# The second layer's raw weight staging and the mixed-tile stores moved from SyncE's queue to GpSimd's, with a fourth staging buffer and later places for what follows them

## The chip, the core and the metric

The kernel runs on one core of one Trainium2 chip. The metric is device time in microseconds (us) of one launch; before the change it is 1452.85 us, the median of three runs (1451.37 to 1453.06). The engines are called as the profile calls them: PE (TensorE matmul, PEld its weight loads), DVE (VectorE), ACT (ScalarE), POOL (GpSimd) and SP (SyncE). SP computes nothing here and only issues DMAs. POOL clears a few tiles and issues the other DMAs. Every engine works through its instructions in order.

## The reference

Three blocks follow one another on a batch of 8 sequences of 576 positions and 512 features.

```python
# 1: attention through 32 packed vectors p, per batch and head (64 features)
p_packed = softmax(scale * p @ k.T) @ v
x = softmax(scale * q @ p_packed.T) @ p_packed
# 2: first feed-forward, x_prev is x one position earlier
xk = mu_k * x + (1 - mu_k) * x_prev ;  xr = mu_r * x + (1 - mu_r) * x_prev
x2 = sigmoid(xr @ w_r) * (relu(xk @ w_k) ** 2 @ w_v)
# 3: positions mixed by a rank-32 product, then the second feed-forward
u = x2 + (x2.T @ U @ V).T
out = u + relu(u @ w_ch1) @ w_ch2          # 512 -> 2048 -> 512
```

The weights arrive as 64-bit floats and are made into 32-bit ones on the chip. Every large product is computed as three products of split parts (a high part and a remainder).

## The kernel before

**How the work is cut.** Attention runs over 16 units (4 batch pairs by 4 head pairs). The first 8 run at the start. The other 8 are woven into the first feed-forward. That feed-forward runs over 12 chunks of 384 positions (`chunks`, numbers 0 to 11): for each, `mix` builds xk and xr on ACT and DVE, `r_block`, `k_block` and `v_block` run the products on PE (tiles `psr`, `psk`, `psv`), and `x2_out` multiplies the result by the gate and stores the mixed tile to DRAM. `attention` is called for four units in chunk 2 and for four in chunk 5; the profile has them from about 215 us to 470 us. The second feed-forward then runs in windows, the first from about 710 us on (tile `psc`). It reads combinations of the weights, prepared earlier, from the DRAM tiles `ws_d` and `t_d` through six `ring` buffers that `load_w` fills from POOL's queue.

**The casts of the second layer's weights.** `Cast.run` is used for 2 pieces of V, 16 of `w_ch1` and 16 of `w_ch2`, from chunk 2 on, at class 3. One cast takes a `st` buffer of three and loads 512 KB of 64-bit numbers into it (the load waits for the buffer's former user). ACT then takes absolute values into tile `a` (L233), and six DVE instructions follow: a maximum on `a`, a shift into tile `m` (L264), two bit operations, a scaling of the low half into `m` (L273) and a sum into `m` (L254). Last, the 32-bit piece in `m` is stored to DRAM (`w1_d`, `w2_d`; V's go to `v_d`). There are two `m` buffers, so the shift of cast number k + 2 waits until the store of cast k has landed. Later `raw_pair` loads these pieces again, `make_ws` and `make_t` build the combinations from them, and `make_t` also runs in the first window.

**What sets the order.** The program is first recorded as operations, then `Plan.emit` places them one after another by its own estimates of times: on each engine it takes what is ready, lower class first. The finish that it assumes for a DMA is what decides where the instructions that wait for it stand on DVE, ACT and PE:

```python
clock[e] = t + (issue if e == "sp" else 1000.0)
dge = max(dge, t + issue) + gap
wire = max(wire, dge + 700.0) + dur * share
op.fin = wire + land
```

The order is fixed by this before the kernel runs, and on the chip each engine keeps it whatever happens. A DMA issue that waits for data holds up every later issue of its queue. Before the change SP issues nearly all DMAs: the attention inputs `kin`, `qin` and `vin`, the chunks' inputs, the `st` loads, and the stores of `m`, of the attention outputs and of the mixed tiles. POOL issues 308 ring loads and 16 loads of raw pieces, from 679 us on.

**Names in the profile.** The profile leaves the numbers in names out: `x_d<-x` is the store of a mixed tile, `w_d<-m` the store of a cast piece, `w_d` under `raw` its later load, `st<-in_moe_w_ch_dram` the load of a cast. `th` is the last factor of an attention unit, `pp` a tile in its middle.

Of the kernel before, what the change touches and what calls it, by code (L numbers as in the profile page):

```python
# [11 lines left out]
I32 = mybir.dt.int32  # L12
# [77 lines left out]

class Op:
    __slots__ = ("engs", "fn", "cls", "seq", "preds", "succs", "left", "end", "eng", "cost", "done", "fin", "name",
                 "group", "vt")

    def __init__(self, engs, fn, cls, seq, cost):
        self.engs, self.fn, self.cls, self.seq, self.cost = engs, fn, cls, seq, cost
# [4 lines left out]
class Plan:  # L101
# [210 lines left out]
            return self.size(o) + 100.0  # L312
        return self.add((eng,), fn, (), (out,))

    def dma(self, out, in_, cls=None, after=(), eng="sp"):
        def fn():
            o = out.get() if isinstance(out, Ref) else out
            i = in_.get() if isinstance(in_, Ref) else in_
            (self.nc.sync if eng == "sp" else self.nc.gpsimd).dma_start(out=o, in_=i)  # L319
            runs = []  # L320
            for ap in (o, i):
                n, dims = 4, list(ap.ap)
                while dims and dims[-1][0] * 4 == n:
                    n *= dims.pop()[1]
                runs.append(n)
            return o.shape[0] * self.size(o) * 4 / (358.0 if min(runs) >= 512 else 180.0)
        return self.add((eng,), fn, [in_] if isinstance(in_, Ref) else [],
                        [out] if isinstance(out, Ref) else [], cost="dma", cls=cls, after=after)


    LAT = {"pe": {"act": 197.0, "dve": 197.0, "pool": 224.0},
# [14 lines left out]
    def emit(self):  # L346
# [68 lines left out]
        while True:  # L415
            best = None
            for e in names:
                for q in (avail[e], pend[e]):
                    while q and q[0][-1].done:
                        heapq.heappop(q)  # L420
                if avail[e]:
                    t = clock[e]
                elif pend[e]:
                    t = max(clock[e], pend[e][0][0])
                else:
                    continue
                if best is None or t < best[0]:
                    best = (t, e)
            grant = None
            for i, (ready, op) in enumerate(asks):  # L430
                for b in op.group:
                    if b.free is not None:
                        t = max(ready, b.free)
                        key = (t, op.cls, op.seq, b.free)
                        if grant is None or key < grant[0]:
                            grant = (key, i, op, b)
            if grant is not None and (best is None or grant[0][0] <= best[0]):
                key, i, op, b = grant
                del asks[i]
                op.vt.bank, op.done, op.eng, op.fin = b, True, "", key[0]  # L440
                b.free, b.last = None, 0.0
                op.fn()
                finish(op)
                continue
            if best is None:
                break
            t, e = best
            q = pend[e]
            while q and q[0][0] <= t:
                ready, _, op = heapq.heappop(q)  # L450
                if op.done:
                    continue
                key = op.seq if e in ("pe", "sp") else ready
                heapq.heappush(avail[e], (op.cls, key, op.seq, op))
            while avail[e] and avail[e][0][-1].done:
                heapq.heappop(avail[e])
            if not avail[e]:
                continue
            op = heapq.heappop(avail[e])[-1]
            op.done, op.eng = True, e  # L460
            dur = op.fn(e) if op.cost == "eng" else op.fn()
            if op.cost == "dma":
                issue, gap, share, land = self.LEAD if t < self.CHUNKS else self.LOADED
                clock[e] = t + (issue if e == "sp" else 1000.0)
                dge = max(dge, t + issue) + gap
                wire = max(wire, dge + 700.0) + dur * share
                op.fin = wire + land
            else:
                if e == "act" and op.cost in ("exp", "sig") and op.cost != table:
                    dur += 1300.0  # L470
                    table = op.cost
                if e == "pe":
                    tick = int(t // self.TICK)
                    if done.get(tick - 1, 0.0) < 3060.0:
                        dur = 2.0 * dur - 3.0
                    tick = int((t + dur) // self.TICK)
                    done[tick] = done.get(tick, 0.0) + self.cols
                clock[e] = t + (max(dur - self.OVER.get(e, 0.0), 0.0) if t < self.AHEAD else dur)
                op.fin = t + dur
            finish(op)  # L480
# [4 lines left out]
def packed_attention_moe_mixer_kernel(  # L485
# [20 lines left out]
    P = 128  # L506
    DM = H * D
# [18 lines left out]
    plan = Plan(nc)  # L526
# [362 lines left out]
    class Cast:  # L889
        N = 512  # L890

        def __init__(self, es, side):
            self.st = Pool(obj=open_pool(es, "cvst", 3, side), bufs=3)
            self.tp = Pool(obj=open_pool(es, "cvtp", 2, side), bufs=2)
            self.pools = [self.st, self.tp]

        def run(self, srcs, n, put=None, parts=None, after=()):
            N = self.N
            raw = srcs[0][1].dtype != F32
            st = plan.tile(self.st, [P, N * 2], I32, "st", parts=tuple(range(len(srcs))))  # L900
            for i, (rows, src) in enumerate(srcs):
                s = st.at(i)
                to = s[rows, 0:2 * n] if raw else s[rows, 0:n].bitcast(F32)
                if raw:
                    src = src.bitcast(I32)
                if src.shape[0] > P:
                    to = to.rearrange("p (a c) -> p a c", a=src.shape[0] // P)
                    src = src.rearrange("(a p) c -> p a c", p=P)
                plan.dma(to, src, after=after)
            if not raw:  # L910
                if parts is None:
                    put(st.bitcast(F32))
# [224 lines left out]
    def x2_out(n, t):  # L1137
        b, c = chunks[n]
        i = 3 * c + t
        x2 = plan.tile(x2_p, [P, 512], F32, "x2")  # L1140
        plan.tt(x2, vps[n][t], rt.pop((n, t)), mul)
        plan.dma(x2_d[b].at(i)[:, i * DM:(i + 1) * DM], x2)
        return x2

    def xu_block(tiles):
# [61 lines left out]
    def raw_pair(src, f):  # L1207
        r = []
        for m in (2 * f, 2 * f + 1):
            t = plan.tile(st_p, [P, 512], F32, "s", name="raw")  # L1210
            plan.dma(t, src[m])
            r.append(t)
        return r

# [363 lines left out]
    CAST0, NPER, NPLAINB, FIRST_T = 2, 5, 1, 10  # L1578
    for m in range(MC):
        def put1(w, m=m):  # L1580
            plan.dma(w1_d[m], w)
        casts.append((slice(0, P), w_ch1[:, m * P:(m + 1) * P], 512, put1))
    for m in range(MC):
        def put2(w, m=m):
            plan.dma(w2_d[m], w)
        casts.append((slice(0, P), w_ch2[m * P:(m + 1) * P, :], 512, put2))

    def finish(n):
# [164 lines left out]
```

## Time and profile before

| what | value |
|---|---|
| median of the runs | 1452.85 us (1451.37 to 1453.06) |
| the profiled execution's own time | 1451.24 us |
| its span | 1449.0 us |
| PE busy | 1405.5 us, 97% |
| DVE busy | 1069.9 us, 74% |
| ACT busy | 700.8 us, 48% |
| POOL busy | 173.8 us, 12%, 340 instructions |
| hardware DMA queue (SP's issues) | 165296 packets, 171.77 MB, 40.2% of 16 engines |
| software DMA queue (POOL's issues) | 45632 packets, 165.70 MB, 38.2% of 16 engines |

PE is busy nearly all the time, so the end comes earlier only where PE waits less or runs faster. A busy share says nothing on that; the waits of PE and what released them do. A wait is listed with the engine and instruction that waited, and after the arrow with what came last. An engine that waits off PE's path costs nothing by itself, so a wait on DVE or ACT counts only as far as PE waits for its result.

### The profile page before, as it was taken

What the parts mean: (1) busy time and instruction counts of PE and PEld (TensorE: products, weight loads), DVE (VectorE), ACT (ScalarE), POOL (GpSimd) and SP (SyncE); (2) the same over time, 40 slices, a digit from 0 to 9 for tenths busy, and PEclk for the clock granted to TensorE, in tenths of its full rate; (3) what the DMA queues carried; (4) which work ended last, traced back from release to release, by engine and by line L of the source; (5) the groups of instructions that cost most, each with busy time, mean ns of one, the idle gap of its engine ahead of it and who ended that gap; (6) DMA issues with size and microseconds to landing.
All of it is one profiled execution on the core that took longest, in us unless ns stands there. A gap on an engine that the chain in (4) does not pass through costs nothing.

```text
span 1449.0 us, 25125 instructions
## 1 busy us (share of the span) xinstructions
PE 1405.5 (97%) x9256; PEld 1273.4 (88%) x9256; DVE 1069.9 (74%) x2071; ACT 700.8 (48%) x1403; POOL 173.8 (12%) x340
## 2 busy tenths in 40 slices
PE   7889998999999999999999999999999999999998
PEld 5558887887887888888898899999999999999997
DVE  6777965887887888878568756957876894696484
ACT  5667654766666666667325322422432342243232
POOL 0000000000000000000121122222222222222221
PEclk8889999999999999999999999999999999999999
DMA  8864335656655466887688799899999989999886
GB/s 232 233 194 145 110 94 135 186 160 184 185 145 175 139 226 237 286 294 231 188 277 258 229 339 293 273 288 305 310 272 303 329 242 330 298 262 288 253 252 176
DMA packets 211050, 339.07 MB, mean 234 GB/s; under 512 B 88304, under 2 KB 120880, under 8 KB 210928
## 3 DMA queue, kind: packets, MB, share of 16 engines
q1 hardware_dynamic: 165296, 171.77, 40.2%
q0 software_dynamic: 45632, 165.70, 38.2%
q8 instruction: 74, 1.21, 0.4%
q14 instruction: 48, 0.39, 0.1%
HBM read 262.87 MB, written 74.52 MB: 233 GB/s over the span
## 4 chain that ended last, share of the span: by engine, by line
PE 67%; issue 15%; DMA 7%; POOL 4%; DVE 3%; ACT 2%; SPq 1%; POOLq 0%; DVEq 0%; ACTq 0%
PE psc L197 17%; PE psv L197 12%; PE psk L197 12%; PE psr L197 7%; PE psat L197 4%; POOL ring L319 4%; PE psX L197 4%; PE psY L197 3%; PE psZ L197 2%; DMA ring<-ws_d 2%; PE psat L209 2%; DMA kin<-in_k_dram 1%; PE psW L197 1%; PE psu L197 1%; DMA w_d<-m 1%
## 5 line engine op out<-in xcount | busy, mean ns | idle before, releaser
L197 PE MATMUL psc<-ob,ring 128*128 128x384 f32 x2016 | 357.0, 335 | 2.2 <-DVE hid L254 0.9
L197 PEld LDWEIGHTS psc<-ob,ring 128*128 128x128 f32 x2016 | 349.6, 188 | 7.8 <-issue 2.7
L197 PE MATMUL psv<-w,kk 128*128 128x512 f32 x783 | 202.7, 396 | 2.3 <-DVE kk L291 2.3
L254 DVE TENSOR_TENSOR hid<-p,psc 128x384 f32<-128x384 f32 x144 | 79.1, 550 | 140.3 <-PE psc L197 140.1
L197 PEld LDWEIGHTS psv<-w,kk 128*128 128x128 f32 x783 | 144.2, 188 | 30.7 <-DVE kk L291 2.7
L288 ACT ACTIVATE p<-psc 128x384 f32<-128x384 f32 x96 | 47.2, 492 | 252.7 <-PE psc L197 247.9
L319 POOL DMA_DIRECT2D ring<-ws_d x168 | 88.9, 529 | 446.6 <-PE psc L197 244.3
L288 ACT ACTIVATE sp<-hid 128x768 fp32r<-128x768 f32 x104 | 87.9, 846 | 109.2 <-PE psX L197 54.3
L254 DVE TENSOR_TENSOR sp<-hid,sp 128x768 fp32r<-128x768 f32 x104 | 99.2, 954 | 25.4 <-ACT sp L288 25.3
L197 PE MATMUL psk<-xk,w 128*128 128x384 f32 x528 | 104.7, 341 | 0.1
L319 POOL DMA_DIRECT2D ring<-t_d x140 | 73.9, 528 | 229.3 <-PE psY L197 65.3
L197 PEld LDWEIGHTS psk<-xk,w 128*128 128x128 f32 x528 | 93.4, 189 | 5.5 <-issue 0.8
L197 PE MATMUL psX<-ring,sp 128*128 128x256 f32 x720 | 88.6, 283 | 0.8 <-DMA ring<-t_d 0.8
L197 PEld LDWEIGHTS psX<-ring,sp 128*128 128x128 f32 x720 | 87.4, 192 | 1.6 <-DMA ring<-t_d 1.6
L197 PE MATMUL psY<-ring,sp 128*128 128x256 f32 x720 | 88.0, 283 | 0.0
L197 PE MATMUL psZ<-ring,sp 128*128 128x256 f32 x720 | 88.0, 283 | 0.0
L197 PEld LDWEIGHTS psY<-ring,sp 128*128 128x128 f32 x720 | 87.1, 192 | 0.0
L197 PEld LDWEIGHTS psZ<-ring,sp 128*128 128x128 f32 x720 | 87.1, 192 | 0.0
L197 PE MATMUL psr<-wA,xr 128*128 128x512 f32 x315 | 86.9, 405 | 0.0
L233 ACT ACTIVATE sp<-hid 128x768 fp32r<-128x768 f32 x52 | 44.0, 846 | 78.7 <-PE psY L197 26.3
L233 ACT ACTIVATE sq<-psk 128x384 f32<-128x384 f32 x96 | 46.5, 488 | 62.0 <-PE psk L197 61.0
L197 PEld LDWEIGHTS psr<-wA,xr 128*128 128x128 f32 x315 | 58.8, 192 | 14.1 <-DVE xr L291 0.8
(202 smaller groups left out, 2400.1 us busy)
## 6 DMA issues: line engine op xcount, KB each, us to landing
ring<-ws_d POOLq DMA_DIRECT2D x168, 512.0 KB, 5.9
ring<-t_d POOLq DMA_DIRECT2D x140, 512.0 KB, 4.8
st<-in_moe_w_ch_dram SPq DMA_DIRECT2D x32, 512.0 KB, 4.9
ws_d<-bl SPq DMA_DIRECT2D x56, 256.0 KB, 3.5
t_d<-bl SPq DMA_DIRECT2D x56, 256.0 KB, 3.5
x_d<-xo SPq DMA_DIRECT2D x16, 576.0 KB, 3.5
x_d<-x SPq DMA_DIRECT2D x36, 256.0 KB, 2.3
kin<-in_k_dram SPq DMA_DIRECT2D x32, 256.0 KB, 5.0
```

The lines of the kernel that those rows point to most:

```text
L197: self.nc.tensor.matmul(o, l, r, start=start, stop=stop, **k)
L209: self.nc.tensor.transpose(out.get(), in_.get(), ident.get())
L233: self.nc.scalar.activation(o, in_.get(), func, **k)
L254: return self.elem(engs, lambda e, o, x, y: e.tensor_tensor(out=o, in0=x, in1=y, op=op), out, [a, b], self.TT, cls)
L288: self.nc.scalar.activation(o, i, AF.Copy)
L319: (self.nc.sync if eng == "sp" else self.nc.gpsimd).dma_start(out=o, in_=i)
```

## The change

In `Op` and `Plan.dma` a number `slack` is added that the planner adds to the finish it assumes for the DMA. On the chip nothing waits for it; what depends on the DMA is placed later. It is 4000 ns for the loads of the casts and for the stores of `w1_d` and `w2_d` pieces. For `raw_pair` it is given as 0, which changes nothing. Every fourth of these casts takes its staging buffer from the pool `xs_p` (one buffer, until then used for `u` tiles only), so there are four in turn. The casts' loads, the stores of the pieces, and the stores of the mixed tiles in `x2_out` are issued by POOL instead of SP. The stores of V's two pieces stay on SP.

```diff
-    def dma(self, out, in_, cls=None, after=(), eng="sp"):
+    def dma(self, out, in_, cls=None, after=(), eng="sp", slack=0.0):
...
+        op.slack = slack
+        return op
...
-                op.fin = wire + land
+                op.fin = wire + land + op.slack
...
+            self.count = 0
...
-            st = plan.tile(self.st, [P, N * 2], I32, "st", parts=tuple(range(len(srcs))))
+            self.count += raw and plan.cls == 3
+            pl, tag = (xs_p, "xs") if plan.cls == 3 and self.count % 4 == 0 else (self.st, "st")
+            st = plan.tile(pl, [P, N * 2], I32, tag, parts=tuple(range(len(srcs))), name="st")
...
-                plan.dma(to, src, after=after)
+                plan.dma(to, src, after=after, slack=4000.0 if plan.cls == 3 else 0.0, eng="pool" if plan.cls == 3 else "sp")
...
-        plan.dma(x2_d[b].at(i)[:, i * DM:(i + 1) * DM], x2)
+        plan.dma(x2_d[b].at(i)[:, i * DM:(i + 1) * DM], x2, eng="pool")
...
-            plan.dma(t, src[m])
+            plan.dma(t, src[m], slack=0.0)
...
-            plan.dma(w1_d[m], w)
+            plan.dma(w1_d[m], w, slack=4000.0, eng="pool")
...
-            plan.dma(w2_d[m], w)
+            plan.dma(w2_d[m], w, slack=4000.0, eng="pool")
```

36 stores of mixed tiles, 34 loads of casts and 32 stores of pieces change the queue: 102 issues leave SP and stand on POOL. What this does to the order is shown at three places. Numbers behind names are tile numbers and differ between the two programs.

The first place is chunk 2, where the first attention unit of the second group is loaded. SP before, from the loads of the next unit's keys on (`x2_d0` is a mixed-tile store, `st` a cast's load, `v_d` the store of a piece of V):

```order
L319 DMA kin_2692<-in_k_dram 128x2x256 x2
L319 DMA kin_2692<-in_k_dram 64x2x64 x2
L319 DMA qin_2693<-in_q_dram 32x18x32 x8
L319 DMA x2_d0_69<-x2_2673 128x512
L319 DMA vin_2741<-in_v_dram 128x2x256
L319 DMA vin_2741<-in_v_dram 64x2x64
L319 DMA vin_2741<-in_v_dram 128x2x256
L319 DMA vin_2741<-in_v_dram 64x2x64
L319 DMA st_2800<-in_moe2_w_ch1_dram 128x4x256
L319 DMA st_2804<-in_moe2_w_ch1_dram 128x4x256
L319 DMA v_d_77<-m_2442 32x288
L319 DMA v_d_77<-m_2483 32x288
```

SP after, at the same place:

```order
L319 DMA kin_2691<-in_k_dram 128x2x256 x2
L319 DMA kin_2691<-in_k_dram 64x2x64 x2
L319 DMA qin_2692<-in_q_dram 32x18x32 x8
L319 DMA vin_2738<-in_v_dram 128x2x256
L319 DMA vin_2738<-in_v_dram 64x2x64
L319 DMA vin_2738<-in_v_dram 128x2x256
L319 DMA vin_2738<-in_v_dram 64x2x64
L319 DMA v_d_77<-m_2442 32x288
L319 DMA v_d_77<-m_2483 32x288
```

And POOL after, where before the change there was nothing between two clearings of `x` tiles (`st_1904` is the first load into the fourth buffer):

```order
L319 DMA x2_d0_69<-x2_1905 128x512
L319 DMA st_2399<-in_moe2_V_dram 32x576
L319 DMA st_2487<-in_moe2_V_dram 32x576
L319 DMA st_2488<-in_moe2_w_ch1_dram 128x4x256
L319 DMA st_1904<-in_moe2_w_ch1_dram 128x4x256
L319 DMA x2_d0_69<-x2_2663 128x512
L319 DMA x2_d0_69<-x2_2669 128x512
L319 DMA x2_d0_69<-x2_2674 128x512
```

The two `w_ch1` loads stand side by side and ahead of the stores, and the stores of V's pieces follow the attention loads directly.

The second place is chunk 6, where the inputs of the last attention unit are loaded. SP before, with the store of a cast piece behind the attention loads and the mixed-tile stores:

```order
L319 DMA kin_5056<-in_k_dram 128x2x256 x2
L319 DMA kin_5056<-in_k_dram 64x2x64 x2
L319 DMA qin_5057<-in_q_dram 32x18x32 x8
L319 DMA x2_d1_70<-x2_4565 128x512
L319 DMA x_5135<-x_d2_67 128x4x512
L319 DMA x2_d1_70<-x2_4586 128x512
L319 DMA x2_d1_70<-x2_4589 128x512
L319 DMA w1_d13_91<-m_4771 128x512
```

POOL after, with the store of the same piece:

```order
L319 DMA x2_d1_70<-x2_4595 128x512
L319 DMA x2_d1_70<-x2_4602 128x512
L319 DMA x2_d1_70<-x2_4605 128x512
L319 DMA st_5171<-in_moe2_w_ch2_dram 128x1024
L319 DMA w1_d13_91<-m_4757 128x512
L319 DMA st_5224<-in_moe2_w_ch2_dram 128x1024
L319 DMA w1_d14_92<-m_4811 128x512
```

The store now has only stores of finished mixed tiles and one cast load ahead of it, and no attention load.

The third place is the start of the first window, with the ring loads (`ws_d0` to `ws_d5`) on POOL. Before:

```order
L319 DMA ring_7883<-ws_d0_94 128x1024
L319 DMA ring_7884<-ws_d1_95 128x1024
L319 DMA ring_7885<-ws_d2_96 128x1024
L319 DMA raw_7971<-w2_d0_122 128x512
L319 DMA raw_7996<-w2_d2_124 128x512
L319 DMA ring_7984<-ws_d3_97 128x1024
L319 DMA ring_8003<-ws_d4_98 128x1024
L319 DMA ring_8004<-ws_d5_99 128x1024
```

After:

```order
L319 DMA w2_d15_137<-m_7445 128x512
L319 DMA ring_7972<-ws_d0_94 128x1024
L319 DMA ring_7973<-ws_d1_95 128x1024
L319 DMA ring_7985<-ws_d2_96 128x1024
L319 DMA raw_8143<-w2_d0_122 128x512
L319 DMA raw_8155<-w2_d2_124 128x512
L319 DMA x2_d3_72<-x2_7815 128x512
L319 DMA x2_d3_72<-x2_7820 128x512
L319 DMA x2_d3_72<-x2_7829 128x512
L319 DMA ring_8152<-ws_d3_97 128x1024
L319 DMA ring_8163<-ws_d4_98 128x1024
L319 DMA ring_8164<-ws_d5_99 128x1024
```

The stores of the last chunk's three mixed tiles now stand between the third and the fourth ring load.

## Rows read from the trace of the kernel before

**Rows 1.** PE's waits from 190 to 740 us: total us, times, longest.

```profile
PE psat L197 <- ACT th L233: 5.2, 1, 5.2
PE psv L197 <- DVE kk L291: 2.3, 1, 2.3
PE psat L209 <- DVE pp L270: 2.1, 1, 2.1
PE psk L197 <- ACT sq L233: 0.8, 2, 0.4
PE psat L197 <- ACT ppt L288: 0.6, 1, 0.6
```

**Rows 2.** Waits of ACT and DVE for DMAs, 190 to 500 us.

```profile
ACT a L233 <- DMA st<-in_moe_w_ch_dram: 11.6, 4, 6.7
DVE m L264 <- DMA w_d<-m: 10.5, 5, 4.0
```

**Rows 3.** SP's issues in chunk 2, in order of time: start, us, instruction.

```profile
211.91 0.44 SPq L319 DMA_DIRECT2D st<-in_moe_w_ch_dram  x1
216.57 0.34 SPq L319 DMA_DIRECT2D x_d<-x  x1
...
238.49 1.09 SPq L319 DMA_DIRECT2D st<-in_moe_w_ch_dram  x2
239.67 0.92 SPq L319 DMA_DIRECT2D v_d<-m  x2
```

**Rows 4.** ACT and DVE in order of time, 243 to 246 us, idle time in brackets.

```profile
243.99 0.66 ACT L233 ACTIVATE a<-st 128x512 f32<-128x512 f32 x1 [6.71 <-DMA st<-in_moe_w_ch_dram]
...
245.61 0.43 DVE L264 TENSOR_SCALAR m<-a 128x512 int32<-128x512 int32 x1 [0.42 <-DMA v_d<-m]
```

**Rows 5.** Busy behind PE's longest wait: length, PE, PEld, DVE, ACT, POOL, clock.

```profile
249.30:253.00 3.70, 3.64 (x13) 3.55 (x14) 3.55 (x7) 1.47 (x5) 0.00 (x0) 0.56 0.00 0
```

**Rows 6.** DVE and SP in order of time, 329 to 341 us.

```profile
329.14 0.69 DVE L254 TENSOR_TENSOR m<-m,a 128x512 f32<-128x512 f32 x1
...
336.27 0.67 SPq L319 DMA_DIRECT2D w_d<-m  x1
...
340.98 0.43 DVE L264 TENSOR_SCALAR m<-a 128x512 int32<-128x512 int32 x1 [2.87 <-DMA w_d<-m]
```

**Rows 7.** DVE and SP in order of time, 434 to 447 us.

```profile
434.36 1.28 DVE L254 TENSOR_TENSOR m<-m,a 128x512 f32<-128x512 f32 x2
...
437.53 0.85 SPq L319 DMA_DIRECT2D w_d<-m  x1
...
446.57 0.43 DVE L264 TENSOR_SCALAR m<-a 128x512 int32<-128x512 int32 x1 [3.95 <-DMA w_d<-m]
```

**Rows 8.** Busy times by stretch, chunks 7 and 11, and the sum over chunks 7 to 11.

```profile
489.40:533.30 43.90, 43.90 (x221) 38.37 (x220) 38.61 (x83) 31.41 (x65) 0.00 (x0) 1.00 0.64 208
...
665.30:710.00 44.70, 44.70 (x240) 38.19 (x238) 30.78 (x66) 25.75 (x58) 4.40 (x8) 1.00 0.69 221
sum 220.60, PE 220.60 PEld 191.20 DVE 176.75 ACT 145.01 POOL 4.51; mean PE 44.12 PEld 38.24 DVE 35.35 ACT 29.00 POOL 0.90
```

**Rows 9.** By tile: POOL's ring-load issues and the w_d stores' landing, min/median/max.

```profile
L319 POOL DMA_DIRECT2D ring<-ws_d x168: 527/527/667, 679.2 to 1369.3; - x168
...
DMA to landing us min/median/max: 2.0/4.3/9.0
```

**Rows 10.** DMA issues by line: KB each, median us from issue to landing.

```profile
ring<-ws_d POOLq DMA_DIRECT2D x168, 512.0 KB, 5.9
st<-in_moe_w_ch_dram SPq DMA_DIRECT2D x32, 512.0 KB, 4.9
...
raw<-w_d POOLq DMA_DIRECT2D x16, 256.0 KB, 4.8
```

**Rows 11.** SP and PE in order of time, at the first window's start.

```profile
707.40 1.68 SPq L319 DMA_DIRECT2D x_d<-x  x3
...
710.08 29.22 PE L197 MATMUL psc<-ob,ring 128*128 128x384 f32 x167
```

More of the change, by code (lines that the diff above doesn't have):

```diff
@@ L92 @@
     __slots__ = ("engs", "fn", "cls", "seq", "preds", "succs", "left", "end", "eng", "cost", "done", "fin", "name",
-                 "group", "vt")
+                 "group", "vt", "slack")
     def __init__(self, engs, fn, cls, seq, cost):
@@ L326, in fn @@
             return o.shape[0] * self.size(o) * 4 / (358.0 if min(runs) >= 512 else 180.0)
-        return self.add((eng,), fn, [in_] if isinstance(in_, Ref) else [],
-                        [out] if isinstance(out, Ref) else [], cost="dma", cls=cls, after=after)
+        op = self.add((eng,), fn, [in_] if isinstance(in_, Ref) else [],
+                      [out] if isinstance(out, Ref) else [], cost="dma", cls=cls, after=after)
+        op.slack = slack
+        return op
     LAT = {"pe": {"act": 197.0, "dve": 197.0, "pool": 224.0},
```

## The prediction

> **What bounds the kernel now.** PE does, so I look for the time in which PE waits or runs slowly, and only then at who released it. The waits of PE from the start of chunk 2 to the first window come first [rows 1]: 5.2, 2.3, 2.1, 0.8 and 0.6 us, 11.0 in all. From chunk 7 on PE is busy in all of 220.60 us [rows 8], so nothing can be won there, and what is won before it moves everything behind it forward. Ahead of chunk 2 the order is the same in both programs.
>
> Next I follow each wait back by the order of time. **The 5.2 us** (PE waits for `th`): ACT had stood for 6.71 us in front of a cast's absolute value, waiting for its load [rows 4]. That load was issued on SP at 238.49 [rows 3], behind the loads of two attention units. DVE, which needs ACT's result, stood as well. PE's clock fell with the wait: in the 3.70 us behind it the granted clock is 0.56 of full speed [rows 5], that is mostly at 1.2 instead of 2.4 GHz. This costs 3.70 x 0.44 = 1.6 us more. **The 2.1 us** (PE waits for `pp`): DVE finished a cast piece at 329.14 + 0.69 = 329.8, SP issued its store at 336.27, and it had landed when DVE went on at 340.98 after 2.87 us of waiting [rows 6]. Of the 11.2 us, 6.4 are SP's queue and 4.7 the transfer. **The 2.3 us** (PE waits for `kk`): the same with the last piece ready by 435.6, issued at 437.53 and landed at 446.57; DVE waited 3.95 us [rows 7]. Here the transfer takes 9.0 us, the longest of the stretch [rows 9]. **The 0.6 us** is put down to ACT, which waited for cast loads four times, 11.6 us in all [rows 2]; I count it as the same kind. The 0.8 us are two short waits of `psk`, behind no DMA, and stay.
>
> So DMAs of the casts are behind 5.2 + 2.3 + 2.1 + 0.6 = 10.2 us, and 1.6 of slow clock: **11.8 us**. PE loses less than the engine that waits for the DMA: 5.2 of 6.71, 2.3 of 3.95, 2.1 of 2.87. A remaining wait on DVE or ACT under 1.5, 1.6 or 0.8 us would therefore cost PE nothing.
>
> **The change, part by part.**
>
> Loads of casts. The second `w_ch1` load now takes the fourth buffer and stands on POOL right behind the first, which was issued at 211.91 [rows 3]; ACT wants it at 243.99 - 6.71 = 237.3. That is 25 us for a load of 4.9 us [rows 10]. Over all casts I counted, in the order, DVE instructions from the moment at which the load can be issued to the cast's first DVE instruction: 9 to 75 before, with eight loads under 20; after, the `w_ch` loads have 27 to 104. One DVE instruction takes 43.90 / 83 = 0.53 us of the stretch at its densest [rows 8], so 27 are 14 us. POOL's issue of this piecewise load isn't in the trace. Its contiguous issues take 0.527 us at the median and 0.667 at most [rows 9]; with four times as many pieces I bound it by 0.5 and 2.1 us (four times 0.527) and take 1. Either way it fits into 14 us, and the wait ends.
>
> Stores of pieces. From a piece's last DVE instruction to the shift that reuses its buffer the order has 9 to 40 DVE instructions before, median 18; after 13 to 48, median 24. While attention runs the shortest are 13, three times 17, and 18. Thirteen are 6.9 us and 17 are 9.0. No store by POOL is in the trace. Below, it is 0.5 + 2.0 us, above 0.5 + 9.0 [rows 9]; POOL's loads of the same 256 KB take 4.8 [rows 10], which are nearest in engine and size, so I take 0.5 + 4.8 = 5.3. Then no store is late. At 9.5 DVE waits 2.6 us at the one place and 0.5 at three, and PE loses 1 to 2.
>
> Stores of V's pieces. They stay on SP, and DVE needs them right where the 5.2 us were: even after that wait it stood 0.42 us more for them [rows 4]. Issued at 239.67 and landed at 245.6, they took 5.9. Ahead of them SP loses what the change moves: it had stood from 212.35 to 216.57 in front of a mixed-tile store, 4.2 us [rows 3], and three such stores and two cast loads at 0.55 (half of the 1.09) are 2.7. So they are issued at 239.67 - 6.9 = 232.8 and land at 238.7; DVE gets there about when ACT did, at 237.3. The wait of 1.4 us is within the 1.5 that cost nothing. If only the issues are saved and not the 4.2, they land at 242.9, and PE loses 5.6 - 1.5 = 4.1 of its 5.2 again.
>
> Mixed-tile stores. On SP 36 issues fewer; on POOL the next cast's store or load waits in order until the mixed tile is there. I included this in the counts above. The clearing of `x` tiles stands behind three such stores twice, over 50 DVE instructions ahead of its use; no cost.
>
> The ring at the first window's start. Three ring tiles instead of six are loaded ahead. The fourth now stands behind the last mixed-tile stores, which SP could issue from 707.40 to 709.1 [rows 11]. With POOL's 0.53 behind the last, the ring load starts by 709.6 and lands 5.9 later [rows 10], at 715.5. PE needs it after 36 matmuls of 29.22 / 167 = 0.175 us, two of which the order puts ahead of 710.08: 710.08 + 5.9 = 716.0. No wait, but only 0.5 us in hand. At a landing of 9 us it would be 2.6. I take 0.3.
>
> Casts later. Counted between the mixed tiles of successive chunks, the casts per chunk hardly move; DVE gets 11 and 12 more instructions in chunks 10 and 11. At 0.53 that is 6 us each, and in chunk 11 DVE is idle for 44.70 - 30.78 = 13.9 us [rows 8]. This hides them; without it up to 6 us would go to PE.
>
> What is late next: the attention unit's own chain through PE, ACT and DVE, of which the 0.8 us are all that shows now. For waits that the new order makes I set another 0.8.
>
> **A rule against the change.** POOL's issues took 527 ns at the median and at the minimum, while DVE was at work [rows 9]. The Trainium skill (SBUF — State Buffer, "SBUF: two separate sides" and the section behind it) says that GpSimd cannot write its DMA descriptors while DVE holds their shared port, and gives some 620 ns alone against 3100 ns beside a DVE copy. By that figure a store would take 3.1 + 4.8 = 7.9 us, about 1 us too late at the one place with 13 instructions, and the sum would lose no more than 1 us. The 667 ns at most in 168 issues don't bear it out.
>
> **The sum.** 11.8 - 0.3 - 0.8 = 10.7 us. The profiled execution took 1451.24, so it would be 1440.5. Its like, the median of three, is 1.6 higher, 1452.85, and I forecast that less 10.7: **1442.2 us**.
>
> **The rivals.**
> - Part of the gain: V's store lands late (4.1 lost) and POOL's stores take near 9 us (1 to 2 lost): 10.7 - 5.6 = 5 left, 1448. For it: V's store is not moved, and one store did take 9.0. Against: the 4.2 us in which SP stood still.
> - Nothing: the waits on DMAs go, but the new order puts DVE or ACT instructions of the casts ahead of the attention chain at other places, and waits as large come back; 1450 to 1454. For it: three waits of 2 to 5 us came from so few places. Against: every distance to a DMA that I counted grew, and [rows 1] show only 0.8 us behind no DMA.
> - Slower: POOL's queue as a whole delivers late. If a store takes 12.5 us, DVE waits at seven places of 13 to 20 instructions while attention runs: 12.5 - 0.53 x count, summed 23 us, less 1.3 hidden at each, 14 us on PE. That exceeds the 10.7: 1456. It decides from about 12 us on. Against: medians of 4.8 and 5.9 on that queue [rows 10].
> - The change not doing what it says is excluded: the order shows the moves.
>
> **How the numbers follow.** Forecast, 1439 to 1446: 0.67. Part, 1446 to 1450: 0.18. Nothing: 0.09. Slower: 0.06. The range reaches from 1438.5 (all 11.8, the 0.8 of psk and a little more) to 1450, which leaves out the last two cases. A measurement here can tell about 0.2%, or 2.9 us, from no change: faster 0.85, same 0.09, slower 0.06.
>
> **What would show it.** Right: PE's waits from 190 to 490 us add up to 1 to 2.5 us, no DVE wait for `w_d<-m`, no ACT wait for a cast's load, the clock full behind 249 us, and `psc` starting 10 to 11 us earlier with the second half as long as before. Wrong: a DVE wait for `v_d` over 1.5 us, POOL stores landing over 9 us after issue, a PE wait for a ring load at the first window, or new waits of PE in chunks 10 and 11.

## The result, and the profile after

| | before | after |
|---|---|---|
| median of the runs | 1452.85 us (five runs beside those of after, 1446.61 to 1455.70) | 1438.22 us (1434.94 to 1444.33, five runs) |
| profiled execution: time, span | 1451.24, 1449.0 us | 1438.22, 1436.5 us |
| PE's waits from 190 to 740 us | 11.0 us | 0.6 us |
| chunk 2 (first `psr`) to the first window (first `psc`) | 510.32 us | 500.84 us |
| first `psc` to the last block of `psW`, near the end | 724.23 us | 721.73 us |

The ratio is 0.9907 with a 95% interval of 0.9884 to 0.993: the changed kernel is 0.9% faster, or 13.5 us of 1452.85. The forecast was 10.7 us and 1442.2; the ratio makes 1439.3 of the median before. The raw median, 1438.22, lies 0.3 us below the low end, 1438.5; the ratio's time lies within.

Single executions of either kernel differ by 9 us, and a part of this arises ahead of chunk 2, where all kernels here have the same order: that part ends between 194.6 and 199.6 us in all profiles but one. So I compare two stretches of the profiles, from the first `psr` of chunk 2 to the first `psc`, and from there to the last block of `psW` (72 matmuls). The table of busy time by stretch (PE, granted clock, DMA share, GB/s) for the kernel before:

```profile
198.63:708.95 510.32, 499.34 (x3038) 1.00 0.64 196
708.95:1433.18 724.23, 721.28 (x4793) 1.00 0.96 281
```

And for the kernel after:

```profile
198.09:698.93 500.84, 500.08 (x3037) 1.00 0.64 195
698.93:1420.66 721.73, 720.49 (x4792) 1.00 0.98 286
```

The first stretch is 9.5 us shorter and the second 2.5. In the first PE now does nearly nothing but work: 500.08 of 500.84 us. It also is busy 0.7 us longer than before, although the slow clock is gone; this comes back below.

PE's waits from 190 to 740 us of after, which answer to [rows 1], are one:

```profile
PE psat L197 <- ACT th L233: 0.6, 1, 0.6
```

The granted clock behind it, where [rows 5] showed 0.56: first in 4 us right behind it (length, busy PE, clock, DMA share, GB/s), then in 100 us (length, busy PE, PEld, DVE, ACT, POOL, clock, DMA share, GB/s):

```profile
248.00:252.00 4.00, 4.00 (x24) 1.00 0.00 0
...
250.00:350.00 100.00, 100.00 (x705) 83.93 (x704) 82.97 (x181) 67.27 (x146) 15.84 (x25) 1.00 0.65 188
```

No DVE wait for `w_d<-m` and no ACT wait for a cast's load is left from 190 to 500 us; [rows 2] had 10.5 and 11.6 us. POOL in chunk 2, in order of time (start, us, instruction, idle before):

```profile
206.56 1.57 POOL L319 DMA_DIRECT2D st<-in_moe_w_ch_dram  x2
216.29 1.74 POOL L319 DMA_DIRECT2D x_d<-x  x3 [8.16 <-DVE x L254]
225.19 0.76 POOL L319 DMA_DIRECT2D st<-in_moe_w_ch_dram  x1 [7.16 <-DVE m L273]
256.17 0.54 POOL L319 DMA_DIRECT2D w_d<-m  x1 [30.22 <-DVE m L254]
```

Both `w_ch1` loads leave from 206.56 on, where the second left SP at 238.49 [rows 3]. POOL now stands in front of what isn't ready, up to 30 us, and nobody waits behind it. SP at the same place, and then DVE:

```profile
210.12 10.52 SPq L319 DMA_DIRECT2D qin<-in_q_dram  x8
...
226.03 9.34 SPq L319 DMA_DIRECT2D qin<-in_q_dram  x8
235.47 2.60 SPq L319 DMA_DIRECT2D vin<-in_v_dram  x4
238.17 1.00 SPq L319 DMA_DIRECT2D v_d<-m  x2
```

```profile
240.44 0.43 DVE L264 TENSOR_SCALAR m<-a 128x512 int32<-128x512 int32 x1 [3.24 <-DMA v_d<-m]
```

The stores of V's pieces leave only 1.5 us earlier than before, and DVE waits 3.24 us for them. PE's 0.6 us follow from that, as the run v1 below shows.

### The profile page after: what moved, and what is told of

Read it like the earlier page. It is cut to its first block, busy times and chain, and to the rows that moved or that the text cites. A ratio compares the mean times of both kernels' runs of the same rounds, so it can differ in the third digit from the quotient of the medians.

```text
span 1436.5 us, 25196 instructions
## 1 busy us (share of the span) xinstructions
PE 1405.2 (98%) x9256; PEld 1273.1 (89%) x9256; DVE 1073.0 (75%) x2077; ACT 700.6 (49%) x1397; POOL 234.4 (16%) x442
## 4 chain that ended last, share of the span: by engine, by line
PE 61%; issue 23%; POOL 7%; DMA 3%; DVE 2%; SPq 1%; ACT 1%; POOLq 0%; DVEq 0%; ACTq 0%
PE psv L197 13%; PE psk L197 13%; PE psc L197 12%; POOL ring L319 7%; PE psr L197 7%; PE psat L197 4%; PE psX L197 2%; PE psZ L197 2%; PE psY L197 2%; PE psat L209 2%; SPq L319 1%; PE psu L197 1%; DMA kin<-in_k_dram 1%; PE psW L197 1%; DMA qin<-in_q_dram 1%
## 5 line engine op out<-in xcount | busy, mean ns | idle before, releaser
L288 ACT ACTIVATE p<-psc 128x384 f32<-128x384 f32 x96 | 47.2, 492 | 251.9 <-PE psc L197 247.2
L254 DVE TENSOR_TENSOR kk<-sq,kk 128x384 fp32r<-128x384 f32 x87 | 48.1, 553 | 30.8 <-ACT kk L288 30.2
```

Source lines behind the costliest of these rows:

```text
L254: return self.elem(engs, lambda e, o, x, y: e.tensor_tensor(out=o, in0=x, in1=y, op=op), out, [a, b], self.TT, cls)
L288: self.nc.scalar.activation(o, i, AF.Copy)
```

## The experiments

Twelve kernels were run. In seven of them every instruction of PE, ACT and DVE stands exactly where it stood in the kernel before (q1, l1, w1, xo, sx) or after (q2, v1), and only the engine that issues some DMAs is another: the planner lays out the program with one queue and the DMA is then issued on the other (a parameter `real`). This parts the queue from the order. b2 keeps b1's order in the same way. In the others the planner makes its own order.

| run | what it is | ratio to before (95%) | PE waits 190 to 740, us | chunk 2 to `psc`, us | `psc` to last `psW`, us |
|---|---|---|---|---|---|
| before | | 1 | 11.0 | 510.3 | 724.2 |
| after | queue, slack, buffer | 0.9907 (0.9884 to 0.993) | 0.6 | 500.8 | 721.7 |
| q1 | before, queue alone | 0.9897 (0.987 to 0.9924) | 1.0 | 498.9 | 723.6 |
| q2 | after's order, all on SP | 0.9959 (0.994 to 0.9978) | 3.3 | 504.3 | 722.2 |
| l1 | before, cast loads on POOL | one run | 10.7 | 513.8 | 722.4 |
| w1 | before, piece stores on POOL | one run | 8.0 | 507.7 | 722.4 |
| xo | before, mixed-tile stores on POOL | one run | 3.7 | 502.8 | 726.5 |
| sx | before, both kinds of stores on POOL | 0.9917 (0.9888 to 0.9946) | 2.8 | 500.0 | 723.9 |
| s0 | after without slack | 0.9937 (0.9914 to 0.996) | 1.7 | 499.7 | 726.1 |
| b1 | after with three buffers | 1.0026 (1.0007 to 1.0046) | 12.4 | 498.7 | 738.8 |
| b2 | b1, raw loads on SP | 1.0 (0.9974 to 1.0025) | 6.0 | 498.7 | 739.6 |
| s1 | before with slack | 1.002 (0.9993 to 1.0047) | 5.2 | 503.7 | 729.8 |
| f1 | before with fourth buffer | 0.9976 (0.996 to 0.9992) | 6.1 | 508.2 | 722.1 |
| v1 | after, V's stores on POOL too | one run | 0 | 499.4 | 723.3 |

Each kernel has one profile. In the six kernels with before's order PE's work in the first stretch agrees to 0.7 us: 497.3 to 498.0 us, when half of the time that PE was busy at a granted clock of 0.50 is taken off. What their stretches differ by beyond this is waits and slow clock.

The theory was that SP's order of issue cost the time (Q); the first rival, that the later places and the buffer are what helps (O).

**q1, the queue alone.** The four kinds of DMA get `real="pool"` in the kernel before:

```diff
-                plan.dma(to, src, after=after)
+                plan.dma(to, src, after=after, real="pool" if plan.cls == 3 else None)
...
-            plan.dma(w1_d[m], w)
+            plan.dma(w1_d[m], w, real="pool")
```

and so `w2_d` and the mixed tiles.

> The kernel before with only the queue changed: the loads of the casts, the stores of the w1/w2 pieces and the mixed-tile stores are issued on POOL, while every instruction of PE, ACT and DVE stands where it stood before (same order, three staging buffers, no slack). Theory Q (what cost the time was that SP issues in order): the second w_ch1 load leaves by 226 us instead of 238.5, so the 5.2 us wait goes; pieces are stored some 5.3 us after they are ready, against 4.8 to 6.4 us (9 to 12 DVE instructions of 0.53 us) at the closest places, so the 2.1 and 2.3 us go nearly; some loads have only 6 to 13 instructions (3 to 7 us) ahead of their use and leave small waits. PE waits from 190 to 740 us add up to 2 to 4 us instead of 11.0; time 1441 to 1444. Theory O (what helps is the later place and the fourth buffer): PE waits of 8 us or more stay, time 1448 to 1452.

PE's waits from 190 to 740 us, and PE's first stretch:

```profile
PE psk L197 <- ACT sq L233: 0.8, 2, 0.4
PE psr L197 <- ACT xr L288: 0.2, 1, 0.2
```

```profile
195.72:694.62 498.90, 497.91 (x3037) 1.00 0.65 200
```

The 0.8 us of `psk`, which were behind no DMA, are there as before [rows 1]; everything else is gone. The clock is at 1.00 in all of 240 to 260 us. The stretch is 11.4 us shorter: 10.0 of it are waits and 1.4 are PE's busy time, 497.91 us against 499.34. The run beat its own forecast of 1441 to 1444, and its ratio can't be told from that of the whole change. Theory O falls: the queue alone gives the gain.

**q2, the order alone.** After, with `real="sp"` on the same DMAs.

> The kernel after with all moved DMAs back on SP, while every instruction of PE, ACT and DVE stands where it stands in the kernel after (slack, fourth buffer and later places kept). Theory Q: the second w_ch1 load is early, but the stores of V's pieces stand again behind mixed-tile stores and attention loads, land at 244 to 247 us and are wanted at 237, so a PE wait of 3 to 6 us stays there, and stores of pieces held up by up to 6 us on SP plus 4.7 to land exceed 13 to 18 DVE instructions (6.9 to 9.5 us) at some places: PE waits of 5 to 9 us from 190 to 740 us, time 1445 to 1450. Theory O: PE waits of 3 us or less, time 1438 to 1441.

What remains of PE's waits, and of DVE's:

```profile
PE psat L197 <- ACT th L233: 3.3, 1, 3.3
```

```profile
DVE m L264 <- DMA v_d<-m: 5.9, 1, 5.9
```

Its 1443.17 us lies between the two theories. The place of V's stores is as Q said, but no piece's store was late: the later places cover SP's delay. So order and queue are two cures for the same waits: the queue ends 10.0 of the 11.0 us, the order alone 7.7. In the stretch the order brings 6.0 us against the queue's 11.4. It misses V's stores, which it doesn't move, and behind the wait that they leave the granted clock is 0.50 from 249.2 to 252.6 us.

**Which DMAs matter: l1, w1, xo, sx.** Each is q1 with only one kind moved, or two.

> The kernel before, every engine's order kept, with only the 34 loads of the casts issued on POOL; stores of pieces and of mixed tiles stay on SP. Measured by PE's waits from 190 to 740 us (11.0 before, 1.0 with all three kinds on POOL) and by the stretch from the first psr of chunk 2 to the first psc (510.3 us before, 498.9 with all three). Theory A (each kind ends its own waits): the second w_ch1 load is early, but V's stores still stand behind mixed-tile stores and attention loads and land at 244 to 246 us, so 3 to 5 us of the 5.2 stay; the 2.1 and 2.3 behind stores of pieces stay: PE waits of 7 to 9.5 us, stretch 506 to 509 us. Rival L (the loads are the cause of the longest wait and of the slow clock): the 5.2 us and the 1.6 us of slow clock go, PE waits 4 to 5 us, stretch 502 to 504 us.

> The kernel before, every engine's order kept, with only the 32 stores of the w1/w2 pieces issued on POOL. Theory A: the waits of 2.1 and 2.3 us go and the 5.2 stays: PE waits of 5.5 to 7 us, stretch from the first psr of chunk 2 to the first psc 505 to 507 us. Rival L: the same here. Rival X (the mixed-tile stores that block SP are behind all of it): the pieces' stores gain, but nothing else moves, as in A; the difference is in the other two runs.

> The kernel before, every engine's order kept, with only the 36 mixed-tile stores issued on POOL. Theory A: SP no longer stands 4.2 us in chunk 2 in front of a mixed tile that isn't ready, and has some 2 us of issues less there; the second w_ch1 load and V's stores come 4 to 6 us earlier, so of the 5.2 us 0 to 2 stay; in the other two places the store of the piece comes 1 to 3 us earlier, and 1 to 3 of the 4.4 us stay: PE waits of 2 to 6 us, stretch 501 to 506 us. Rival X (this kind alone is behind it): PE waits under 2.5 us, stretch 499 to 501 us. Rival L: PE waits of 9 us or more, stretch over 508 us.

> The kernel before, every engine's order kept, with the stores of the pieces and the mixed-tile stores issued on POOL, the loads of the casts left on SP. Theory A (a store that waits for data is what holds SP up; a load that waits for a buffer hardly does): with both kinds of stores gone the loads leave SP in time; PE waits from 190 to 740 us of 0.8 to 2.5 us, stretch from the first psr of chunk 2 to the first psc 498.5 to 501 us (498.9 with the loads moved too), time 1435 to 1443. Rival L (the loads have to leave SP too): ACT waits for cast loads stay at 5 us or more and PE loses 2 to 4 us to them, stretch 501 to 504 us, time 1441 to 1446.

PE's waits in l1:

```profile
PE psv L197 <- DVE kk L291: 4.4, 1, 4.4
PE psat L209 <- DVE pp L270: 3.6, 1, 3.6
PE psat L197 <- DMA vin<-in_v_dram: 1.5, 1, 1.5
```

in w1, with ACT's wait for cast loads from 190 to 500 us:

```profile
PE psat L197 <- ACT th L233: 4.6, 1, 4.6
PE psat L197 <- ACT ppt L288: 1.9, 1, 1.9
```

```profile
ACT a L233 <- DMA st<-in_moe_w_ch_dram: 12.6, 4, 5.8
```

and in xo, with SP's issues in chunk 2:

```profile
PE psat L209 <- DVE pp L270: 2.2, 1, 2.2
PE psk L197 <- ACT sq L233: 0.8, 2, 0.4
PE psv L197 <- DVE kk L291: 0.7, 1, 0.7
```

```profile
211.13 5.64 SPq L319 DMA_DIRECT2D qin<-in_q_dram  x8
...
232.48 1.09 SPq L319 DMA_DIRECT2D st<-in_moe_w_ch_dram  x2
233.67 0.92 SPq L319 DMA_DIRECT2D v_d<-m  x2
```

In w1 the two waits behind stores of pieces fall from 4.4 to 0.7 us and the 5.2 falls only to 4.6, as theory A said. Another wait grows from 0.6 to 1.9, so that the sum of 8.0 and the stretch of 507.7 lie a little above its ranges.

In xo the 5.2 us are gone, though loads and V's stores are still on SP: they leave 6 us earlier (4.7 counted from the start of chunk 2). Waits and stretch are inside theory A's ranges, and rival X, with waits under 2.5 us, falls. The stretch is 7.5 us shorter, the largest part of q1's 11.4. The mixed-tile stores were thus the worst of what held SP, a store that waits for data with everything behind it.

In l1 the 5.2 us are nearly gone, and theory A, which had 3 to 5 of them stay, missed. But the waits behind stores grew from 4.4 to 8.0 us, which no theory expected: DVE waits 15.9 us for `w_d<-m` there against 10.5 [rows 2]. That the casts, no longer held up by their loads, reach the late stores sooner would explain it, but this is only argued. PE's waits in all hardly change, 10.7 us against 11.0; the stretch grew from 510.3 to 513.8 because the clock fell behind both of these waits (length, busy PE, clock, DMA share, GB/s):

```profile
343.50:350.30 6.80, 5.44 (x18) 0.50 0.33 94
456.10:462.90 6.80, 4.95 (x12) 0.50 0.44 135
```

Half of the 5.44 and 4.95 us, 5.2 us, went to the slow clock, against 1.6 in before. The run's one time, 1458.2, also holds a first part that ended 5 us later than the others (203.9).

In sx the stretch comes within 1.1 us of q1's, and the run's time, 1438.4, is inside theory A's range. ACT still waits 6.0 us for cast loads, as rival L had it, but PE loses only 2.8 us in all, just above A's 2.5. So with the stores gone the loads bring 1.8 us of waits and 1.1 us of the stretch; the two ratios, 0.9917 and 0.9897, can't be told apart.

**The slack and the buffer: s0, b1, f1, s1, b2.**

> The kernel after with the slack set to 0, POOL's queue and the fourth buffer kept; the planner makes its own order. The shortest distances of stores to the shift that waits for them fall from 13 to 10 or 11 DVE instructions (5.3 to 5.8 us), about what a store by POOL takes. Theory Q: DVE waits of under 1 us at three or four places, hidden; PE waits of 190 to 740 us under 3 us, time 1437 to 1442. Rival O: waits of DVE and PE of 2 to 4 us come back at two or more places, time 1443 to 1447.

s0 (every `slack=0.0`) came out at 1441.29 us, with 1.7 us of PE's waits and 499.7 us in the first stretch, as theory Q said; its ratio can't be told from after's. Its second stretch was 4.4 us longer than after's. I don't read a cause into that, since xo, whose order is before's, shows as much.

> The kernel after without the fourth staging buffer (three in turn), the rest kept; the planner makes its own order from that. Theory Q: the second w_ch1 load waits for the buffer of V's first piece, which DVE leaves at 226 us, is issued on POOL at about 227 and lands at 234, ahead of the 237 at which ACT wants it, and the later loads have 9 to 60 DVE instructions: no PE wait over 1 us comes back, time within 0.2% of the kernel after, 1436 to 1441. Rival B (the fourth buffer is what ended the longest wait): a wait of ACT for a cast load and 3 to 6 us of PE come back, time 1442 to 1446.

```diff
-            pl, tag = (xs_p, "xs") if plan.cls == 3 and self.count % 4 == 0 else (self.st, "st")
+            pl, tag = (xs_p, "xs") if plan.cls == 3 and self.count % 4 == 9 else (self.st, "st")
```

This is the surprise: 1454.5 us, slower than before, and by neither theory's mechanism. No cast is late in chunks 2 to 6. The loss is at the first window. POOL in order of time:

```profile
696.79 1.74 POOL L319 DMA_DIRECT2D x_d<-x  x3 [4.38 <-DVE x L254]
709.24 1.22 POOL L319 DMA_DIRECT2D raw<-w_d  x2 [10.71 <-DVE bl L254]
710.45 1.61 POOL L319 DMA_DIRECT2D ring<-ws_d  x3
```

and PE:

```profile
718.07 17.17 PE L197 MATMUL psc<-ob,ring 128*128 128x384 f32 x85 [9.10 <-DMA ring<-ws_d]
```

POOL stood 10.71 us in front of two raw loads that waited for buffers, with ring loads behind them. The head of line has moved from SP to POOL. The same two loads leave 24 us ahead of the first `psc` in before and in q1 (684.9 and 670.5 us), 4.0 us ahead in after (694.9), and 10.9 us behind it in b1. The buffers come free late because DVE's work on them is placed late. DVE in b1:

```profile
707.01 0.55 DVE L254 TENSOR_TENSOR hid<-p,psc 128x384 f32<-128x384 f32 x1
...
708.28 1.09 DVE L254 TENSOR_TENSOR bl<-sums,bl 128x256 fp32r<-128x256 f32 x3
```

In b1 these `bl` stand behind the first `hid` of the window; in after they are done at 695.1 us and that `hid` starts at 702.18. The casts are later, too. By the traces the last cast's last DVE instruction stands 111 instructions ahead of the first `hid` in before, 113 in s0, 54 in after, 46 in b1 and 37 in s1 (the expectations count rows of the order and come to a few less). So the slack pushes the casts towards the window, and the fourth buffer takes some of that back. But the count alone doesn't decide: s1 has the fewest, and its two raw loads leave 10.7 us ahead of the first `psc`.

PE also ran slowly behind the wait: the granted clock is 0.50 from 712.5 to 722.7 us, where PE was busy for 4.63 us, so 2.3 of them are the clock's.

> The kernel after with three staging buffers, as in the run b1, with one further edit: in the first window the 16 loads of raw w2 pieces are issued on SP, not on POOL; every engine's order is that of b1. Theory R: b1 lost its time because POOL stood 10.71 us in front of two raw loads that waited for their buffers, with the ring loads behind them, so PE waited 9.1 us for a ring load at 718 us; without the raw loads ahead of it the ring load leaves at about 699, and the wait falls under 1 us: time 1439 to 1445, the stretch from the first psc to the first psX 187 to 190 us instead of 200.9. Rival B (the missing buffer costs it elsewhere, or the ring itself comes too late): the wait stays at 5 us or more, time 1448 to 1455.

POOL and PE in b2:

```profile
701.32 0.77 POOL L319 DMA_DIRECT2D ring<-ws_d  x1 [4.53 <-PE psc L197]
```

```profile
715.55 14.63 PE L197 MATMUL psc<-ob,ring 128*128 128x384 f32 x74 [2.67 <-DMA ring<-ws_d]
```

The ring load leaves 7.4 us earlier, counted from the first `psc`, and the wait falls from 9.1 to 2.7 us, so the raw loads were behind most of it, though R had said under 1 us. The time did not follow (1450.39 us, 4.1 under b1 but above the 1439 to 1445 expected): in the profiles the two stretches add up to 0.8 us more than in b1. The second stretch shows where the rest sits. Against after, b1 has 14.0 us more of idle PE there and 2.3 of slow clock, b2 12.1 and 3.4. In both PE waits 2.9 us for ACT and DVE ahead of the ring wait. In b2 a wait of 1.55 us is new in the later windows, another grew from 1.19 to 1.82, and the clock falls to 0.50 twice (705.8 to 709.2 and 716.0 to 719.4 us). So theory R holds for the larger part of the wait and not for the time; why b2's later waits differ from b1's stays open.

> The kernel before with the fourth staging buffer alone, no slack, all on SP. The second w_ch1 load can be issued right behind the first, so ACT no longer waits for it; V's stores stay behind the attention loads on SP, and the pieces' stores have 10 to 14 DVE instructions at ten places. The casts come early (last cast 123 DVE rows ahead of the first hid). Theory: of the 5.2 us 3 to 4 stay (as in the run q2, 3.3), the 2.1 and 2.3 behind pieces' stores stay about as they are, no ring wait at the window: PE waits from 190 to 740 us of 6 to 9 us, time 1446 to 1451. Rival B (the fourth buffer is what ends the waits): PE waits under 4 us, time 1440 to 1444.

> The kernel before with the slack alone: 4000 ns for the loads of the casts and the stores of w1/w2 pieces; all of them stay on SP, three buffers. Counted in the order, the last cast's last DVE instruction stands 32 DVE rows ahead of the first hid of the window (107 in the kernel before, 51 after, 43 in the run b1). Theory W (the slack alone pushes the casts into the start of the window, where POOL waits for a buffer in front of the raw loads with three ring loads behind them): PE waits for ring<-ws_d between 690 and 740 us by 6 to 15 us, the raw loads leave POOL at 705 us or later, and what the later places save in chunks 2 to 6 (3 to 6 of the 11.0 us) is given back: time 1449 to 1459. Rival S (the slack is what helps): waits of PE from 190 to 690 us under 4 us, none at the window, time 1440 to 1445.

f1's waits, PE and DVE:

```profile
PE psat L197 <- ACT th L233: 4.5, 1, 4.5
```

```profile
DVE m L264 <- DMA v_d<-m: 6.8, 1, 6.8
DVE m L264 <- DMA w_d<-m: 5.6, 7, 1.8
```

As expected ACT no longer waits for a cast load, V's stores take its place (4.5 us of PE, somewhat more than I said), and 1446.34 us is inside the range. The waits behind stores of pieces became smaller than expected, 0.5 us on PE. s1 gains in the first stretch (503.7) and gives it back in the second (729.8): no difference to before, as theory W had it, but not at W's place. No ring load was waited for at the first window, where the raw loads left at 691.9 us; the loss of 5.5 us is one wait at the second, 3.9 us, and 1.7 us of slow clock behind it (0.51 from 896.0 to 899.5 us):

```profile
895.98 2.26 PE L197 MATMUL psc<-ob,ring 128*128 128x384 f32 x6 [3.89 <-DVE hid L254]
```

DVE had stood 6.65 us there for ACT, and ACT 4.87 us for a load on SP, `y<-uq_d`, which landed 12.8 us after its issue; in before the same load took 9.6. Each is one execution, and why the load landed late isn't known, so whether the slack has a part in it is not shown.

**v1, V's stores on POOL too.**

```diff
-            plan.dma(v_d[:, c * 288:(c + 1) * 288], w[0:NP, 0:288])
+            plan.dma(v_d[:, c * 288:(c + 1) * 288], w[0:NP, 0:288], real="pool")
```

> The kernel after, every engine's order kept, with the two stores of V's pieces on POOL as well. They stand there behind the third w_ch1 load, which was issued at 225.19 us, so they leave when the pieces are ready, by 226.5 and 228.5 us, and land by 234, ahead of the 237.2 at which DVE wants the buffer. Theory: DVE's wait of 3.24 us for v_d and PE's 0.6 us for th both go, PE waits from 190 to 740 us are 0.5 us or less; the time moves by no more than that, 1436 to 1440 (one run). Rival: the wait for th has another cause (ACT or DVE work that the slack put there), and 0.4 to 1 us of it stay though DVE no longer waits for v_d.

POOL's issues, and PE in the first stretch:

```profile
225.12 0.52 POOL L319 DMA_DIRECT2D v_d<-m  x1 [0.63 <-DVE st L264]
227.16 0.50 POOL L319 DMA_DIRECT2D v_d<-m  x1 [1.53 <-DVE st L281]
```

```profile
197.08:696.49 499.41, 499.41 (x3037) 1.00 0.64 195
```

PE waits for nothing any more between chunk 2 and the window: 499.41 of 499.41 us. The 0.6 us of after were V's stores. The time of the one run, 1437.67, doesn't differ from after's.

## Why the prediction was right, and where it was not

**What bounds the kernel, 11.8 us.** Right, and q1 measures it without any change of order: 11.0 us of waits become 1.0, PE is busy 1.4 us less as the clock no longer falls (1.6 by the prediction), and the stretch is 11.4 us shorter.

**Loads of casts.** Right. The second load stands right behind the first, and POOL's issue of a piecewise load took 0.75 us at the median, within the 0.5 to 2.1 and near the 1 that I took. But l1 and sx show that moving them brings little or nothing.

**Stores of pieces.** Right in size. POOL's issues of `w_d<-m` (min, median and longest ns), and their time to landing in us:

```profile
L319 POOL DMA_DIRECT2D w_d<-m x32: 542/542/687, 256.2 to 667.3; - x32
...
DMA to landing us min/median/max: 2.3/4.8/8.3
```

I took 0.5 + 4.8; it was 0.54 + 4.8, and the longest, 8.3, is under the upper bound of 9.0. Nothing waited for them. With at most 687 ns for an issue, the rule that the prediction weighed (the Trainium skill, SBUF — State Buffer, "SBUF: two separate sides" and the section behind it, some 3100 ns for a DMA beside a DVE copy) did not show here, with DVE busy 82.97 of 100 us between 250 and 350.

**V's stores: the step that failed.** I forecast the issue at 232.8 and the landing at 238.7, with 1.4 us of DVE's wait covered. It was issued at 238.17, landed at 240.4, and DVE waited 3.24 us, over the 1.5 that I had named as a wrong sign. Two errors partly cancelled. I gave SP back the 4.2 us of standing and 2.7 of issues, but SP spent 7.5 us more on `qin`: 10.52 and 9.34 us for eight issues against 6.24 and 6.09 in the kernel before. And the landing took 2.2 us, not 5.9, which was luck. PE lost 0.6 us, less than the 3.24 - 1.5 of the prediction's rule, since the order after puts more matmuls ahead of `th`: PE ran out of work at 247.2 us, in before at 244.2.

**Mixed-tile stores.** I counted their leaving as 36 issues less and one stand of 4.2 us. xo shows them as the largest single part, 7.5 of 11.4 us.

**The ring at the first window.** The step was right, and tighter than I said: I had 0.5 us in hand and put 0.3 down as lost. PE is busy in all of 700 to 750 us, but its weight loads waited for the fourth and the fifth ring load:

```profile
706.11 2.03 PEld L197 LDWEIGHTS psc<-ob,ring 128*128 128x128 f32 x12 [0.19 <-DMA ring<-ws_d]
708.42 1.71 PEld L197 LDWEIGHTS psc<-ob,ring 128*128 128x128 f32 x10 [0.28 <-DMA ring<-ws_d]
```

The fourth left at 700.15 us, behind the last mixed-tile stores, and took the 5.9 us that I had assumed. Nothing was in hand, where in before it had landed 11 us ahead of the first `psc`. By the starts of the matmuls, 0.17 us apart otherwise, PE lost some 0.2 us of the 0.5 (an estimate). What I left out are the raw loads, which also come near: 4.0 us in hand instead of 24.

**Casts later.** They are hidden in chunks 10 and 11 as said, but I priced only DVE's work. b1 shows the real price: with the later places the work on the raw buffers moves into the window as well, and POOL stands in front of it.

**Waits of the new order, 0.8 us.** New waits there are none, and the 0.8 us of `psk`, which were to stay, went as well. But PE is busy 500.08 us in after's first stretch and 497.91 in q1's. With the slow clock taken off it is 499.4 to 500.1 in the three kernels with after's order (after, q2, v1), against the 497.3 to 498.0 of the six with before's. In the groups of PE's work from 190 to 720 us one stands out, 2.7 us, for the same 144 matmuls; after first, then q1:

```profile
L197 PE MATMUL psu<-x,ust 128*64 128x256 f32 x144 | 21.6, 391 | 0.0
```

```profile
L197 PE MATMUL psu<-x,ust 128*64 128x256 f32 x144 | 18.9, 390 | 0.0
```

After's order splits these runs of twelve into pieces among attention matmuls. So the new order costs some 2 us as work, not as waits. That the splitting is the cause is not shown: it was not tried by itself, and s1, whose group takes 20.3 us, has only 497.8 in all.

**The sum.** 11.8 - 0.6 (V) - 2.3 (the order: 500.08 us of work against 499.34 - 1.6) + 0.8 (`psk`) is 9.7; the stretch gave 9.5. The forecast of 10.7 for the whole was passed (12.0 in both stretches together) only by the second one, 2.5 us shorter. v1, with the same order there, has 0.9 of that, so most of it is difference between executions: that the whole came out above the forecast, and not 1.2 us below it, is chance.

**The rivals.** The part and the nothing cases fell. The slower one, POOL delivering after 12.5 us, fell by the 8.3. A slower case through POOL's queue did exist, one edit away: b1, by standing in front of loads, not by late landing.

## What to carry to other kernels

When an in-order queue carries both transfers that others wait for and stores that wait for data, move first the stores that stand longest in front of unfinished data; xo did two thirds of the work with 36 of 102 moves, by its one profile. Then look at what stands behind the moved ones in the new queue, and how long before its use each transfer leaves: raw loads that left 4 us ahead of the window instead of 24 cost nothing, and in the next order, where they left 11 us behind its start, PE waited 9 us. Queue and placement cured the same waits here, so a change that does both should be taken apart before both are kept: q1 has the whole gain without slack or buffer.

## What the runs showed of the hardware

Issues on SP took longer while a load issued by POOL was under way. All issues of `qin` from 200 to 480 us, in after and then in sx, where the cast loads are on SP (min, median and longest ns):

```profile
L319 SPq DMA_DIRECT2D qin<-in_q_dram x64: 560/632/3771, 210.1 to 428.7; - x64
```

```profile
L319 SPq DMA_DIRECT2D qin<-in_q_dram x64: 560/630/1461, 209.3 to 423.9; - x64
```

The eight in chunk 2 took 6.1 to 10.5 us in the four kernels read with cast loads on POOL (after, q1, l1, v1) and 5.6 to 6.2 where they are on SP (before, q2, xo, sx). The shortest of the first kind, l1's 6.1, began when POOL's last load had landed 5 us before. The Trainium skill (DMA: Bandwidth & Descriptors, "Issuing engines are not separate DMA queues") says that transfers run on the same 16 engines whoever started them, and that several issuers save only the time of issue. The first fits these rows, which do not show it by themselves. As to the second, more than the time of issue was saved here: SP had stood 4.2 us in front of one mixed tile whose issue then took 0.34 us [rows 3], and q1's stretch is 11.4 us shorter with as many issues as before.

The landing of one small store depends on what was issued just before it. `v_d<-m`, 36 KB, took 4.0 to 5.9 us on SP right behind a cast load of 512 KB (before, q2, xo, sx), 4.3 to 5.2 us on POOL behind a cast load there (v1), and 1.6 to 2.2 us on SP where the loads were on POOL and had landed (after, q1, l1). No such store was issued on one queue while a load of the other was under way, so these rows don't tell whether the queue matters or only the load.
